# Attention, gated MLP and top-2 experts on one core: TensorE in a fixed order, attention and gate work placed by product count, and a written order for the first four attention tiles

## The chip, the cores and the metric

The kernel runs on one core of a Trainium2 chip. The metric is the device time of one execution in microseconds, as the median of several runs. Five engines work side by side, each through its own list of instructions in order: TensorE (PE; its weight loads are shown apart as PEld), VectorE (DVE), ScalarE (ACT), GpSimd (POOL) and SyncE (SP), whose queue issues nearly all transfers. Engines wait for each other only where data or a buffer demands it.

## The reference, cut to what matters

```python
# attention in chunks of 64: q, k, v are (4, 8, 576, 64)
scores = scale * q_c @ k_c.T;  scores -= scores.max(-1);  attn = exp(scores)
out = (attn / (attn.sum(-1) + 1e-9)) @ v_c          # -> x: 2304 x 512
h = x @ w_in                                        # 512 -> 2048
x = (h * clip(h + 3, 0, 6) / 6) @ w_out             # 2048 -> 512
noisy = x @ w_gate + log1p(exp(x @ w_noise)) * noise
top2, weights = two largest of 8 experts, softmax over the two
out[rows of e] += weight * (relu(x[rows] @ w1[e]) @ w2[e])   # 512 -> 1024 -> 512, e = 0..7
```

## The kernel before, in words

The 2304 tokens are 18 tiles of 128 rows, in five blocks of 4, 4, 4, 3 and 3 tiles (BT). For each block the MLP runs over 16 units of 128 hidden columns. One unit is 12 matmuls into `h` (`s1`, line 230, 512 or 384 columns wide) and 3 matmuls per tile into that tile's accumulator `acc` (`s2`, line 239). Every number is kept as a high and a low part, which is why each product takes three matmuls (PASSES). The `acc` products of unit u are written behind the `h` products of unit u + 1; between them ACT and DVE turn `h` into `r` (L264, L265) and into `g`, high on ACT (L266) and low on DVE (L271).

The MLP weights come as 32 half units of 512 KB in a 64-bit format. During block 0 each half is turned into two float parts: three integer operations on DVE (L141 to L143, into `u`), a copy on ACT (the high part, L145) and a subtraction on DVE (the low part, L154). The even half of a unit is needed by its `h` products, the odd half by its `acc` products.

The attention of a tile is a chain over three engines: scores on PE (`sc`, L166), row maximum on DVE (L168), either eight exponentials with sums on ACT (L174, the form called `acts`) or a subtraction on DVE, one exponential on ACT and a sum on DVE (L176 to L178), the norm on DVE (L183 to L185), four transposes on PE (`pt`, L192) and a copy on ACT (L194), the product with v on PE (`xo`, L209), and the high and low part of the MLP's input on ACT and DVE (L212, L213). Tiles 0 to 3 come ahead of block 0 (the lead phase); the tiles of block b + 1 are worked off during block b. The gate of a tile of the block before is a second chain: transposes (L300), four small products (L309), a transpose (L318), a sum on DVE (L319), and per block a top-2 choice on DVE (`gate_top`) and positions by two small matmuls on PE (`gate_pos`, L369 and L370). The `x2` and `x2e` tiles are what a block hands to its gate. PSUM banks p6 and p7 form the tile `pair`, in which these chains work.

What sets the order: the program is built by a scheduler, which places each engine's instructions by its own estimate of when they can run. Only from block 4 on, up to the second group of expert rows, is TensorE held to the written order (`manual_schedule`). Work beside the MLP is hung in two ways: by unit (`side`), and, in `route`, by `ticks`, a counter that goes up with every 4 `h` matmuls and with every 3 `acc` matmuls. After block 4 come the experts, whose rows are gathered by POOL.

Of the kernel before, what the change touches and what calls it, by code (L numbers as in the profile page):

```python
# [42 lines left out]
def tile_kernel(ctx, tc, qkv, w1u, w2u, wg, noise, out):  # L43
# [115 lines left out]
    def att_a(t, tag, acts=False):  # L159
        qt, kt, vt = st["qkv", t]  # L160
        sc = bank(tag, [P, 8, 64], "sc")
        for c in range(2):
            for hp in range(KD):
                for r in range(2):
                    s = slice(r * 64, r * 64 + 64)
                    nc.tensor.matmul(sc[s, c * KD + hp, :], qt[s, hp, c, :], kt[s, c, hp, :], start=True, stop=True)  # L166
# [4 lines left out]
        if acts:  # L171
            nc.vector.tensor_scalar(mx, mx, -0.125, None, op0=ALU.mult)
            for h in range(8):
                nc.scalar.activation(sm[:, h], sc[:, h], AF.Exp, scale=0.125, bias=mx[:, h], accum_out=su[:, h])  # L174
        else:
            nc.vector.tensor_tensor(sm, sc, mx.to_broadcast([P, 8, 64]), op=ALU.subtract)  # L176
# [20 lines left out]
    def att_c(t):
        b = max(i for i in range(NB) if B0[i] <= t)
        i = t - B0[b]
# [12 lines left out]
        nc.scalar.activation(hi, xo, AF.Copy)  # L212
        nc.vector.tensor_tensor(lo, xo, hi.bitcast(F32), op=ALU.subtract)  # L213
# [289 lines left out]
    warm = bank("p3", [P, 4, P], "warm")  # L503
    for i in range(10):
        nc.tensor.matmul(warm, ones, ones[:, None, :].to_broadcast([P, 4, P]), start=True, stop=True)
# [264 lines left out]
```

## Time and profile before

| | |
|---|---|
| median of 3 runs | 1024.29 us (1023.94 to 1024.99) |
| the profiled execution, own time | 1015.68 us |
| its span, first to last instruction | 1013.9 us |
| its mean granted TensorE clock | 0.966 of full speed |
| DVE, ACT, POOL busy | 434.0, 338.8, 141.9 us |

Times in the rows are microseconds from the start of the span. A timeline row gives start, length, engine, line, operation, the tile written and the tiles read, and a count; equal instructions in a row are merged. In brackets stands how long the engine was idle before, and what released it. The count of small products is doubled or quadrupled there against the program. The length of a group of matmuls overlaps with the next by about 0.1 to 0.4 us, so costs are read from start to start. A row of windows gives, for a stretch, its length, the busy time and number of instructions of each engine, the granted TensorE clock (PEclk) and the use of the DMA engines.

### The profile page before, as it was taken

How to read it: one execution, taken by the hardware profiler on the slowest of the kernel's cores; microseconds unless marked ns; L12 is line 12 of the kernel's file. 1: busy time of each engine (PE TensorE's matmuls, PEld its weight loads, DVE VectorE, ACT ScalarE, POOL GpSimd, SP SyncE). 2: the span in 40 equal slices, each digit the busy share in tenths (PEclk: the TensorE clock that was granted, in tenths of full speed). 3: DMA queues.
4: the chain of work that ended last, by engine and by line, in shares of the span. 5: the costliest groups of instructions: out<-in, count | busy, mean ns of one | idle time of the engine just before them, and what ended most of it. 6: DMA issues, size and time to landing. Idle time of an engine off the chain costs nothing.

```text
span 1013.9 us, 14516 instructions
## 1 busy us (share of the span) xinstructions
PE 958.5 (95%) x5960; PEld 818.6 (81%) x5960; DVE 434.0 (43%) x864; ACT 338.8 (33%) x646; POOL 141.9 (14%) x129
## 2 busy tenths in 40 slices
PE   5699999997999999968999999999999999999995
PEld 3488877775787788857998889898989999999894
DVE  6999542334432343326553343333434343332221
ACT  4355442233222232334552343332333232321110
POOL 0000000000300002004202420221313031130311
PEclk8699999998899999978999999999999999999998
DMA  9555120014910120112531573363736345240412
GB/s 349 197 166 182 64 74 1 32 32 142 275 32 5 48 95 1 32 53 63 155 112 68 101 222 92 110 131 106 131 108 134 105 111 129 74 63 22 52 23 32
DMA packets 37195, 99.46 MB, mean 98 GB/s; under 512 B 9984, under 2 KB 10368, under 8 KB 37120
## 3 DMA queue, kind: packets, MB, share of 16 engines
q1 hardware_dynamic: 27008, 77.43, 24.5%
q0 software_dynamic: 10112, 21.02, 11.6%
q8 instruction: 48, 0.79, 0.3%
q14 instruction: 27, 0.22, 0.1%
HBM read 75.15 MB, written 23.28 MB: 97 GB/s over the span
## 4 chain that ended last, share of the span: by engine, by line
PE 91%; DVE 4%; DMA 1%; ACT 1%; issue 1%; POOL 1%; SPq 0%; POOLq 0%; ACTq 0%
PE h L230 42%; PE acc L239 38%; PE pair L239 3%; PE pair L413 2%; PE pair L166 2%; PE pair L209 1%; PE pair L300 1%; PE pair L309 1%; DMA raw<-in_w1u_dram 1%; PE pair L192 1%; DVE u L142 1%; DVE u L143 0%; POOL table L386 0%; DVE Xa L213 0%; DVE u L141 0%
## 5 line engine op out<-in xcount | busy, mean ns | idle before, releaser
L239 PE MATMUL acc<-w,g 128*128 128x512 f32 x1680 | 430.6, 398 | 0.0
L239 PEld LDWEIGHTS acc<-w,g 128*128 128x128 f32 x1680 | 310.3, 189 | 63.2 <-issue 1.6
L230 PE MATMUL h<-Xa,w 128*128 128x320 f32 (+3 forms) x1344 | 257.6, 341 | 4.5 <-ACT Xa L212 3.8
L230 PEld LDWEIGHTS h<-Xa,w 128*128 128x128 f32 x1344 | 220.2, 192 | 26.3 <-ACT Xa L212 4.3
L118 DVE TENSOR_TENSOR w<-raw,w 128x1024 fp32r<-128x1024 f32 x64 | 78.4, 1226 | 128.7 <-ACT w L117 128.5
L430 DVE SCALAR_TENSOR_TENSOR g<-h,g 128x320 fp32r<-128x320 f32 (+2 forms) x128 | 62.5, 489 | 160.8 <-ACT g L429 160.7
L429 ACT ACTIVATE g<-h 128x320 fp32r<-128x320 f32 (+2 forms) x128 | 56.1, 438 | 201.4 <-PE h L230 201.2
L230 PE MATMUL h<-Xe,w 128*128 128x320 f32 (+1 forms) x672 | 110.3, 316 | 0.0
L265 DVE SCALAR_TENSOR_TENSOR r<-r,h 128x512 f32<-128x512 f32 (+1 forms) x80 | 50.6, 632 | 137.4 <-ACT r L264 137.2
L230 PE MATMUL h<-Xb,w 128*128 128x384 f32 (+1 forms) x480 | 106.8, 366 | 1.4 <-ACT Xb L212 1.4
L230 PEld LDWEIGHTS h<-Xe,w 128*128 128x128 f32 x672 | 103.6, 188 | 2.7
L117 ACT ACTIVATE w<-raw 128x1024 fp32r<-128x1024 f32 x64 | 67.9, 1060 | 100.4 <-PE pair L239 88.1
L264 ACT ACTIVATE r<-h,b 128x512 f32<-128x512 f32 (+1 forms) x80 | 51.6, 645 | 134.2 <-PE h L230 131.2
L230 PEld LDWEIGHTS h<-Xb,w 128*128 128x128 f32 x480 | 85.8, 188 | 13.2 <-ACT Xb L212 1.7
L386 POOL DMA_INDIRECT table<-pay,slot x36 | 36.0, 1000 | 399.8 <-DVE slot L383 390.3
L403 POOL DMA_INDIRECT xr<-x2d,tab x40 | 39.9, 998 | 270.7 <-PE pair L413 252.1
L451 POOL DMA_INDIRECT out_dram<-arena,tab x40 | 63.1, 1576 | 88.0 <-DVE arena L448 68.5
L271 DVE TENSOR_TENSOR g<-r,g 128x512 fp32r<-128x512 f32 (+1 forms) x80 | 50.9, 636 | 38.7 <-ACT g L266 38.0
L266 ACT ACTIVATE g<-r 128x512 fp32r<-128x512 f32 (+1 forms) x80 | 47.2, 590 | 55.7 <-DVE r L265 48.2
L239 PE MATMUL pair<-w,g 128*128 128x512 f32 x144 | 41.7, 395 | 0.0
L239 PEld LDWEIGHTS pair<-w,g 128*128 128x128 f32 x144 | 26.9, 188 | 6.0
L145 ACT ACTIVATE w<-u 128x512 fp32r<-128x512 f32 x32 | 20.1, 632 | 34.0 <-DVE u L143 33.9
(135 smaller groups left out, 527.3 us busy)
## 6 DMA issues: line engine op xcount, KB each, us to landing
raw<-in_w2u_dram SPq DMA_DIRECT2D x64, 512.0 KB, 4.1
raw<-in_w1u_dram SPq DMA_DIRECT2D x24, 512.0 KB, 4.5
arena<-in_qkv_dram SPq DMA_DIRECT2D x14, 768.0 KB, 5.3
out_dram<-zero SPq DMA_DIRECT2D x4, 1536.0 KB, 19.9
rawx<-in_w1u_dram SPq DMA_DIRECT2D x8, 512.0 KB, 8.6
x2d<-x SPq DMA_DIRECT2D x15, 256.0 KB, 2.7
lead<-in_qkv_dram SPq DMA_DIRECT2D x3, 768.0 KB, 9.2
x2d<-zero SPq DMA_DIRECT2D x1, 1536.0 KB, 9.1
```

Source lines behind the costliest of these rows:

```text
L117: nc.scalar.activation(w[:, 0], raw, AF.Copy)
L118: nc.vector.tensor_tensor(w[:, 1], raw, w[:, 0].bitcast(F32), op=ALU.subtract)
L230: nc.tensor.matmul(dst, w[:, a, kd * P:(kd + 1) * P], x[:, b, kd, t0:t0 + n], start=(k == 0), stop=(k == 3 * KD - 1))
L239: nc.tensor.matmul(acc[i], g[:, a, i * P:(i + 1) * P], w[:, b, DM:], start=(first and j == 0), stop=(last and j == 2))
L264: nc.scalar.activation(r, st["h", b], AF.Relu, bias=b3)
L265: nc.vector.scalar_tensor_tensor(r, r, 6.0, st["h", b], op0=ALU.min, op1=ALU.mult)
L266: nc.scalar.activation(st["g", b, u][:, 0], r, AF.Copy)
L271: nc.vector.tensor_tensor(g[:, 1], st["r", b], g[:, 0].bitcast(F32), op=ALU.subtract)
L403: nc.gpsimd.indirect_dma_start(out=xr, out_offset=None, in_=x2d[:rows], in_offset=bass.IndirectOffsetOnAxis(ap=st["tab", key][:, i, 0:1], ...
L429: nc.scalar.activation(g[:, 0, t0:t0 + n], h, AF.Relu)
L430: nc.vector.scalar_tensor_tensor(g[:, 1, t0:t0 + n], h, 0.0, g[:, 0, t0:t0 + n].bitcast(F32), op0=ALU.max, op1=ALU.subtract)
L451: s = nc.gpsimd.indirect_dma_start(out=out, out_offset=bass.IndirectOffsetOnAxis(ap=tab[:, i, 0:1], axis=0), in_=y, in_offset=None, comput ...
```

## The change

The attention and conversion helpers are cut into single steps (`conv_a` into `conv_u` and `conv_hi`, `conv_b` into `conv_lo`, `att_a` into `att_sc`, `att_mx`, `att_e` and `att_n`, `att_b` into `att_pt` and `att_at`, `att_c` into `att_xo`, `att_hi` and `att_lo`). The lead phase is then written out step by step, and PE, DVE and ACT are held to that order among these steps. Between the steps stand 20 more matmuls on constants (`keep_warm`). Only halves 0 and 1 belong to the lead phase now, where there were four; tile 1 takes the exponentials on ACT too; the loads of tiles 1 to 3 go ahead of the first weights. Banks p2 and p5 become a second pair, so that two tiles can have their `xo` at once.

From block 0 on TensorE follows the written order, and the attention and gate steps of blocks 0 to 3 hang on ticks: a tile every 24 ticks (20 where a block has 3 tiles), `pt` 11 ticks behind `sc`, `xo` 4 behind that, the gate of a tile 2, 6 and 9 ticks behind `sc`. DVE, ACT, POOL and SP are still ordered by the scheduler after the lead phase. In the changed file the lines stand further down: L142 to L144 and L159 are the conversion on DVE, L177 to L201 the softmax, L248 the low part of the MLP's input, L305 and L311 `r` and the low part of `g`, L270 and L279 the `h` and `acc` products, L171, L214 and L235 `sc`, `pt` and `xo`, L340, L349 and L358 the gate's steps on PE, L409 and L410 `gate_pos`; `pair_69` and `pair_70` are the two pairs.

```diff
...
-    pair = ps.tile([P, 2, DM], F32, name="pair")
+    pairs = [ps.tile([P, 2, DM], F32, name=f"pair{i}") for i in range(2)]
+    in_pair = {"p6": (0, 0), "p7": (0, 1), "p2": (1, 0), "p5": (1, 1)}
     def bank(tag, shape, name):
-        if tag in ("p6", "p7"):
-            t = pair[:, tag == "p7"]
+        if tag in in_pair:
...
+            t = pairs[in_pair[tag][0]][:, in_pair[tag][1]]
...
-    def conv_a(s):
+    def conv_u(s):
...
-        hi = st["w", "m", j][:, 0, h * DM:(h + 1) * DM]
-        nc.scalar.activation(hi, u.bitcast(F32), AF.Copy)
...
+    def conv_hi(s):
+        if s >= 2 * U1:
+            return
+        j, h = divmod(s, 2)
+        nc.scalar.activation(st["w", "m", j][:, 0, h * DM:(h + 1) * DM], st["u", s].bitcast(F32), AF.Copy)
+    def conv_lo(s):
...
-    def att_a(t, tag, acts=False):
+    def att_sc(t, tag):
...
+    def att_mx(t, acts):
+        sc = st["sc", t]
...
+    def att_e(t):
+        sm, su, mx, acts = st["att", t]
+        sc = st.pop(("sc", t))
+        if acts:
             for h in range(8):
                 nc.scalar.activation(sm[:, h], sc[:, h], AF.Exp, scale=0.125, bias=mx[:, h], accum_out=su[:, h])
         else:
-            nc.vector.tensor_tensor(sm, sc, mx.to_broadcast([P, 8, 64]), op=ALU.subtract)
             nc.scalar.activation(sm, sm, AF.Exp, scale=0.125)
+    def att_n(t):
+        sm, su, mx, acts = st["att", t]
+        if not acts:
...
+    def att_a(t, tag, acts):
+        att_sc(t, tag)
+        att_mx(t, acts)
+        att_e(t)
+        att_n(t)
...
+    def att_pt(t, tag):
...
+    def att_at(t, at):
+        nc.scalar.activation(at, st.pop(("pt", t)), AF.Copy)
         st["attT", t] = at
-    def att_c(t):
-        b = max(i for i in range(NB) if B0[i] <= t)
-        i = t - B0[b]
+    def att_b(t, tag):
+        att_pt(t, tag)
+        att_at(t, at_[0])
+    def att_xo(t, pair=0):
...
+    def att_hi(t):
+        nc.scalar.activation(xpart(t, 0), st["xo", t], AF.Copy)
+    def att_lo(t):
+        nc.vector.tensor_tensor(xpart(t, 1), st.pop(("xo", t)), xpart(t, 0).bitcast(F32), op=ALU.subtract)
+    def att_c(t):
+        att_xo(t)
+        att_hi(t)
+        att_lo(t)
...
-    warm = bank("p3", [P, 4, P], "warm")
-    for i in range(10):
-        nc.tensor.matmul(warm, ones, ones[:, None, :].to_broadcast([P, 4, P]), start=True, stop=True)
+    warm = bank("p4", [P, 4, P], "warm")
+    def keep_warm(n):
+        for i in range(n):
+            nc.tensor.matmul(warm, ones, ones[:, None, :].to_broadcast([P, 4, P]), start=True, stop=True)
+    keep_warm(10)
...
-    for c in [0, 10, 1, 2, 11, 3, 12, 13, 14, 15, 16]:
+    for c in [0, 1, 2, 3, 10, 11, 12, 13, 14, 15, 16]:
...
+    with tc.manual_schedule(engines={nc.tensor.engine, nc.vector.engine, nc.scalar.engine}):
+        att_sc(0, "p0"), att_mx(0, True), att_e(0)
+        att_sc(1, "p1"), att_mx(1, True), att_e(1)
+        keep_warm(3)
+        att_n(0), att_pt(0, "p3"), att_at(0, at_[0])
+        att_sc(2, "p0"), att_mx(2, True)
+        keep_warm(3)
+        att_n(1), att_e(2), att_pt(1, "p3"), att_xo(0, 0), att_at(1, at_[1])
+        att_sc(3, "p1"), att_mx(3, False)
+        att_hi(0), att_e(3), att_xo(1, 1)
+        keep_warm(6)
+        conv_u(0)
+        att_lo(0), att_hi(1), conv_hi(0), att_n(2), att_n(3)
+        att_pt(2, "p3"), att_at(2, at_[0]), att_pt(3, "p3"), att_at(3, at_[1])
+        att_lo(1), att_xo(2, 0), att_xo(3, 1)
+        keep_warm(8)
+        conv_u(1), att_hi(2), conv_hi(1), att_hi(3)
+        conv_lo(0), conv_lo(1)
+        att_lo(2), att_lo(3)
+    constants()
     LT = BT[0]
-    HL = 4
-    step = 0
-    for t in range(LT + 2):
-        if t < LT:
-            att_a(t, ("p0", "p1")[t % 2], t % 2 == 0)
-        if 0 <= t - 2 < LT:
-            att_c(t - 2)
-        if t < LT:
-            att_n(t)
-        if 0 <= t - 1 < LT:
-            att_b(t - 1, ("p2", "p5")[t % 2], at_[t % 2])
-        if step < HL:
-            conv_a(step)
-            if step > 0:
-                conv_b(step - 1)
-            step += 1
-        if t == 1:
-            constants()
-    conv_b(step - 1)
...
-                for s in (2 * u + HL, 2 * u + HL + 1):
-                    conv_a(s)
-                    conv_b(s)
+                for s in (2 * u + 2, 2 * u + 3):
+                    conv_u(s)
+                    conv_hi(s)
+                    conv_lo(s)
...
+    order = tc.manual_schedule(engines={nc.tensor.engine})
+    order.__enter__()
     for b in range(NB):
         side = {}
         if b == 0:
             at(side, 6, table_init)
-        elif b < NB - 1:
+        n0 = st.get("tick", 0)
+        every = 24 if BT[b] == 4 else 20
+        if 0 < b < NB - 1:
             t0, nt = GRP[b - 1]
             for i in range(nt):
-                at(side, 4 * i + 1, gate_t, t0 + i, "p7")
-                at(side, 4 * i + 2, gate_m, t0 + i, "p6")
-                at(side, 4 * i + 2, gate_r, t0 + i, "p6")
-            at(side, 4 * nt - 1, gate_top, b - 1)
-            at(side, 4 * nt - 1, gate_pos, b - 1)
+                n = n0 + 8 + every * i
+                at(ticks, n, gate_t, t0 + i, "p7")
+                at(ticks, n + 4, gate_m, t0 + i, "p7")
+                at(ticks, n + 7, gate_r, t0 + i, "p7")
+            at(ticks, n + 8, gate_top, b - 1)
+            at(ticks, n + 22, gate_pos, b - 1)
...
-                u = 4 * i
-                at(side, u, att_a, t, "p6", b == 0)
-                at(side, u, att_n, t)
-                at(side, u + 2, att_b, t, "p7")
-                at(side, u + 3, att_c, t)
+                n = n0 + 6 + every * i
+                at(ticks, n, att_a, t, "p6", b == 0)
+                at(ticks, n + 11, att_b, t, "p7")
+                at(ticks, n + 15, att_c, t)
                 if t + 2 < NTILE:
-                    at(side, u + 3, load_tile, t + 2, bufs[4 + t % 2])
+                    at(ticks, n + 16, load_tile, t + 2, bufs[4 + t % 2])
         if b == NB - 2:
             for j in range(3):
                 at(side, 12 + j, load_raw, U1 + j)
         if b == NB - 1:
-            order = tc.manual_schedule(engines={nc.tensor.engine})
-            order.__enter__()
...
```

TensorE where block 3 ends and block 4 begins (`Xb` is the input of block 3, `Xa` that of block 4), before:

```order
L239 MATMUL acc<-w,g 128x512 x9
L192 MATMUL pair<-ident,arena 128x128 x4
L209 MATMUL pair<-at_93,arena 64x64 x16
L166 MATMUL pair<-arena 64x64 x16
L300 MATMUL pair<-ident,x_2945 128x128 x4
L309 MATMUL pair<-at_94,wg_sb 32x128 x4
L318 MATMUL pair<-ident,lp 128x128
L192 MATMUL pair<-ident,arena 128x128 x4
L209 MATMUL pair<-at_93,arena 64x64 x16
L230 MATMUL h<-Xa,w 128x384
L300 MATMUL pair<-ident,x2e 128x128 x4
L230 MATMUL h<-Xa,w 128x384 x11
```

and changed:

```order
L270 MATMUL h<-Xb,w 128x384 x12
L279 MATMUL acc<-w,g 128x512 x6
L409 LDWEIGHTS upper
L409 MATMUL pair_69<-m,upper 128x32
L410 LDWEIGHTS ones
L410 MATMUL pair_69<-macc,ones 128x32
L279 MATMUL pair_70<-w,g 128x512 x3
L270 MATMUL h<-Xb,w 128x384 x12
L279 MATMUL acc<-w,g 128x512 x6
L279 MATMUL pair_70<-w,g 128x512 x3
L270 MATMUL h<-Xa,w 128x384 x12
L279 MATMUL acc<-w,g 128x512 x6
```

The last `xo` of one tile and the whole of the next tile's attention, with two gates between, stood in a run without MLP products; now the MLP products of both blocks follow each other, and only `gate_pos` stands among them.

VectorE in the lead phase, before (`u` and `w` are weight conversion, the rest attention):

```order
L141 TENSOR_SCALAR u<-raw 128x512
L142 SCALAR_TENSOR_TENSOR u<-raw,u 128x512
L168 TENSOR_REDUCE mx<-sc 128x8
L143 SCALAR_TENSOR_TENSOR u<-raw,u 128x512
L172 TENSOR_SCALAR mx<-mx 128x8
L154 TENSOR_TENSOR w<-u,w 128x512
L168 TENSOR_REDUCE mx<-sc 128x8
L183 TENSOR_SCALAR su<-su 128x8
L176 TENSOR_TENSOR lead<-sc,mx 128x512
L184 RECIPROCAL su<-su 128x8
L141 TENSOR_SCALAR u<-raw 128x512
L185 TENSOR_TENSOR lead<-lead,su 128x512
```

and changed:

```order
L177 TENSOR_REDUCE mx<-sc 128x8
L181 TENSOR_SCALAR mx<-mx 128x8
L177 TENSOR_REDUCE mx<-sc 128x8
L181 TENSOR_SCALAR mx<-mx 128x8
L199 TENSOR_SCALAR su<-su 128x8
L200 RECIPROCAL su<-su 128x8
L201 TENSOR_TENSOR lead<-lead,su 128x512
L177 TENSOR_REDUCE mx<-sc 128x8
L181 TENSOR_SCALAR mx<-mx 128x8
L199 TENSOR_SCALAR su<-su 128x8
L200 RECIPROCAL su<-su 128x8
L201 TENSOR_TENSOR lead<-lead,su 128x512
```

The conversion steps have left this stretch; they come behind the maximum of tile 3.

VectorE late in block 0, around the `r` of unit 10, before:

```order
L142 SCALAR_TENSOR_TENSOR u<-raw,u 128x512
L271 TENSOR_TENSOR g<-r,g 128x512
L142 SCALAR_TENSOR_TENSOR u<-raw,u 128x512
L143 SCALAR_TENSOR_TENSOR u<-raw,u 128x512 x2
L141 TENSOR_SCALAR u<-raw 128x512
L265 SCALAR_TENSOR_TENSOR r<-r,h 128x512
L142 SCALAR_TENSOR_TENSOR u<-raw,u 128x512
L154 TENSOR_TENSOR w<-u,w 128x512 x2
L168 TENSOR_REDUCE mx<-pair 128x8
L143 SCALAR_TENSOR_TENSOR u<-raw,u 128x512
L271 TENSOR_TENSOR g<-r,g 128x512
```

and changed, around the `r` of the same unit:

```order
L142 TENSOR_SCALAR u<-raw 128x512
L143 SCALAR_TENSOR_TENSOR u<-raw,u 128x512 x2
L159 TENSOR_TENSOR w<-u,w 128x512
L144 SCALAR_TENSOR_TENSOR u<-raw,u 128x512 x2
L142 TENSOR_SCALAR u<-raw 128x512
L159 TENSOR_TENSOR w<-u,w 128x512
L143 SCALAR_TENSOR_TENSOR u<-raw,u 128x512
L159 TENSOR_TENSOR w<-u,w 128x512
L305 SCALAR_TENSOR_TENSOR r<-r,h 128x512
L144 SCALAR_TENSOR_TENSOR u<-raw,u 128x512
L248 TENSOR_TENSOR Xb<-pair_69,Xb 128x2x2x128
L311 TENSOR_TENSOR g<-r,g 128x512
```

Ten of the conversion steps that now stand in a row ahead of this `r` are shown; before, four stood between it and the last `g`.

More of the change, by code (lines that the diff above doesn't have):

```diff
@@ L143, in conv_a @@
         nc.vector.scalar_tensor_tensor(u, lo32, 29, u, op0=ALU.logical_shift_right, op1=ALU.bitwise_or)
-        hi = st["w", "m", j][:, 0, h * DM:(h + 1) * DM]
-        nc.scalar.activation(hi, u.bitcast(F32), AF.Copy)
         st["u", s] = u
         load64(s + 7 if s < 10 else s + 3 if s >= 14 else -1)
-    def conv_b(s):
+    def conv_hi(s):
[4 more added lines that the diff above has]
+    def conv_lo(s):
         if s >= 2 * U1:
@@ L166, in att_a @@
                     nc.tensor.matmul(sc[s, c * KD + hp, :], qt[s, hp, c, :], kt[s, c, hp, :], start=True, stop=True)
+        st["sc", t] = sc
+    def att_mx(t, acts):
+        sc = st["sc", t]
         mx = work.tile([P, 8, 1], F32, tag="mx", bufs=2, name="mx")
@@ L172, in att_a @@
             nc.vector.tensor_scalar(mx, mx, -0.125, None, op0=ALU.mult)
+        else:
+            nc.vector.tensor_tensor(sm, sc, mx.to_broadcast([P, 8, 64]), op=ALU.subtract)
+        st["att", t] = (sm, su, mx, acts)
+    def att_e(t):
+        sm, su, mx, acts = st["att", t]
+        sc = st.pop(("sc", t))
+        if acts:
             for h in range(8):
@@ L175, in att_a @@
         else:
-            nc.vector.tensor_tensor(sm, sc, mx.to_broadcast([P, 8, 64]), op=ALU.subtract)
             nc.scalar.activation(sm, sm, AF.Exp, scale=0.125)
+    def att_n(t):
+        sm, su, mx, acts = st["att", t]
+        if not acts:
             nc.vector.tensor_reduce(su, sm, axis=AX.X, op=ALU.add)
-        st["att", t] = (sm, su)
-    def att_n(t):
-        sm, su = st["att", t]
         nc.vector.tensor_scalar(su, su, 1e-9, None, op0=ALU.add)
@@ L185, in att_n @@
         nc.vector.tensor_tensor(sm, sm, su.to_broadcast([P, 8, 64]), op=ALU.mult)
-    def att_b(t, tag, at=None):
+    def att_a(t, tag, acts):
[4 more added lines that the diff above has]
+    def att_pt(t, tag):
         sm = st.pop(("att", t))[0].rearrange("p h k -> p (h k)")
@@ L192, in att_b @@
             nc.tensor.transpose(pt[:, m, :], sm[:, m * P:(m + 1) * P], ident)
-        at = at_[0] if at is None else at
-        nc.scalar.activation(at, pt, AF.Copy)
+        st["pt", t] = pt
+    def att_at(t, at):
+        nc.scalar.activation(at, st.pop(("pt", t)), AF.Copy)
         st["attT", t] = at
-    def att_c(t):
-        b = max(i for i in range(NB) if B0[i] <= t)
-        i = t - B0[b]
+    def att_b(t, tag):
+        att_pt(t, tag)
+        att_at(t, at_[0])
+    def att_xo(t, pair=0):
         at = st.pop(("attT", t))
         qt, kt, vt = st.pop(("qkv", t))
-        xo = pair[:, :, :2 * P].rearrange("p a (j n) -> p a j n", j=2)
+        xo = pairs[pair][:, :, :2 * P].rearrange("p a (j n) -> p a j n", j=2)
         for c in range(2):
@@ L210, in att_c, with xpart @@
                                          at[s, c * 2 + j, r * 64:r * 64 + 64], start=True, stop=True)
-        hi, lo = (xb[b][:, w, :, i * P:(i + 1) * P].rearrange("p (j a) n -> p a j n", a=2) for w in range(2))
-        nc.scalar.activation(hi, xo, AF.Copy)
-        nc.vector.tensor_tensor(lo, xo, hi.bitcast(F32), op=ALU.subtract)
+        st["xo", t] = xo
+    def xpart(t, w):
+        b = max(i for i in range(NB) if B0[i] <= t)
+        i = t - B0[b]
+        return xb[b][:, w, :, i * P:(i + 1) * P].rearrange("p (j a) n -> p a j n", a=2)
+    def att_hi(t):
[6 more added lines that the diff above has]
+        att_lo(t)
     ticks = {}
```

## Prediction

> **What bounds the kernel now.** I read the head of the page first, then stretches of the span by engine, then TensorE's timeline where it is idle.
>
> ```profile
> span 1013.9 us, 14516 instructions
> ...
> PE 958.5 (95%) x5960; PEld 818.6 (81%) x5960; DVE 434.0 (43%) x864; ACT 338.8 (33%) x646; POOL 141.9 (14%) x129
> ...
> PEclk8699999998899999978999999999999999999998
> ```
>
> TensorE is the bound: 55 of 1014 us are without it, and the clock row drops at the start, in the 10th and 11th slice and in the 18th and 19th (each 25.3 us). What is to be won lies there. Everywhere else TensorE runs at these rates:
>
> ```profile
> 71.41 2.77 PE h L230 x12
> ...
> 117.96 2.78 PE acc L239 x12
> ...
> 359.75 4.06 PE L230 MATMUL h<-Xb,w 128*128 128x384 f32 x22
> 363.74 0.43 PE L309 MATMUL pair<-at,wg_sb 128*32 128x128 f32 x8
> ```
>
> 12 products of 512 columns in 2.77 or 2.78 us are 0.231 each; from 359.75 to 363.74 stand 22 of 384 columns, 0.181 each.
>
> First, the lead phase and block 0. The third column group is TensorE, then weight loads, then DVE:
>
> ```profile
> 8.50:21.50 13.00, 7.32 (x136) 6.30 (x136) 11.34 (x26) 7.21 (x36) 0.00 (x0) 0.74 1.03 414
> 21.50:41.60 20.10, 6.94 (x107) 4.99 (x107) 20.10 (x41) 8.69 (x15) 0.00 (x0) 0.57 0.79 290
> 41.60:110.00 68.40, 68.40 (x431) 55.05 (x432) 66.92 (x127) 34.48 (x84) 1.89 (x4) 0.98 0.48 152
> ...
> 110.00:142.10 32.10, 31.43 (x225) 25.12 (x223) 11.49 (x21) 14.48 (x47) 0.00 (x0) 1.00 0.10 31
> ...
> L154 DVE TENSOR_TENSOR w<-u,w x32: 673/682/693, 11.6 to 109.2; 128x512 fp32r<-128x512 f32 x32
> ```
>
> DVE is busy 98.4 of the 101.5 us up to 110 (11.34 + 20.10 + 66.92), where its last weight conversion ends (the last L154 starts at 109.2), and 11.5 of 32.1 us behind that. So up to 110 two engines are at their limit at once from 41.6 on, and DVE alone before. TensorE enters block 0 late and cold:
>
> ```profile
> 1.07 4.45 PE L505 MATMUL warm<-ones 128*128 128x512 bf16 x10 [1.07 <-DVE early L522]
> ...
> 10.40 1.93 PE L166 MATMUL sc<-lead 64*64 64x64 f32 x32 [3.08 <-DMA lead<-in_qkv_dram]
> ...
> 15.87 1.11 PE L192 MATMUL pt<-ident,lead 128*128 128x128 f32 x4
> ...
> 39.65 1.22 PE L230 MATMUL h<-Xa,w 128*128 128x512 f32 x2 [2.33 <-ACT Xa L212]
> 41.58 4.18 PE L230 MATMUL h<-Xa,w 128*128 128x512 f32 x11 [0.71 <-DVE Xa L213]
> ...
> 142.14 3.56 PE L230 MATMUL h<-Xb,w 128*128 128x512 f32 x13 [0.71 <-ACT Xb L212]
> ```
>
> Second, where block 1 ends. From 242.14 to 256.79 no MLP product runs; the steps of one tile's attention wait for each other, and the clock is halved by the time the products return:
>
> ```profile
> 242.14 0.69 PE L209 MATMUL pair<-at,arena 64*64 64x64 f32 x32
> 244.27 1.15 PE L166 MATMUL pair<-arena 64*64 64x64 f32 x32 [1.44 <-DVE Xa L213]
> 246.94 1.12 PE L300 MATMUL pair<-ident,x2e 128*128 128x128 f32 x4 [1.52 <-DVE arena L176]
> ...
> 256.79 4.58 PE L230 MATMUL h<-Xa,w 128*128 128x512 f32 x13 [0.72 <-ACT Xa L212]
> 261.30 1.15 PE L166 MATMUL pair<-arena 64*64 64x64 f32 x32
> ...
> 256.00:260.00 4.00, 3.28 (x12) 2.55 (x9) 0.69 (x1) 0.60 (x1) 3.08 (x4) 0.54 1.02 416
> 260.00:264.00 4.00, 4.00 (x45) 3.14 (x45) 1.83 (x3) 1.32 (x2) 3.09 (x4) 1.00 1.07 391
> ```
>
> Third, the same where block 3 ends, from 431.46 to 469.93, with a second wait in it, for the top-2 choice:
>
> ```profile
> 431.46 0.60 PE L192 MATMUL pair<-ident,arena 128*128 128x128 f32 x4
> ...
> 458.63 0.18 PE L369 MATMUL pair<-m,upper 128*128 128x32 bf16 x1 [3.45 <-DVE m L349]
> ...
> 468.05 0.42 PE L309 MATMUL pair<-at,wg_sb 128*32 128x128 f32 x8 [0.32 <-DVE lgs L319]
> ...
> 469.93 2.34 PE L239 MATMUL acc<-w,g 128*128 128x512 f32 x9
> ...
> 458.00:462.00 4.00, 2.65 (x10) 2.00 (x9) 2.10 (x16) 0.71 (x2) 1.03 (x2) 0.50 0.02 4
> ```
>
> The 3.45 us without work before 458.63 are followed by a halved clock (0.50). The Trainium skill ("TensorE: Matmul & The Clock Gate", "What's actually happening") has the clock fall to half after an idle window of about 3.4 us and come back after a busy one; these rows agree.
>
> **The boundaries.** What the steps cost among products, at full clock, is read from start to start:
>
> ```profile
> 63.01 0.60 PE L192 MATMUL pair<-ident,arena 128*128 128x128 f32 x4
> 63.37 2.57 PE L239 MATMUL acc<-w,g 128*128 128x512 f32 x10
> ...
> 68.66 0.69 PE L209 MATMUL pair<-at,arena 64*64 64x64 f32 x32
> 69.28 2.13 PE L239 MATMUL acc<-w,g 128*128 128x512 f32 x8
> ...
> 76.45 1.15 PE L166 MATMUL pair<-arena 64*64 64x64 f32 x32
> 77.53 0.73 PE L239 MATMUL acc<-w,g 128*128 128x512 f32 x2
> ```
>
> `pt` costs 0.36, `xo` 0.62, `sc` 1.08. A `gate_t` is the same four transposes, 0.36; `gate_m` I put at 0.36 too; the transpose of `gate_r` and `gate_pos` at under 0.1 each.
>
> End of block 1: 242.14 to 261.30 are 19.2 us. In them lie two `xo`, one each of `sc`, `pt`, `gate_t`, `gate_m`, `gate_r` and `gate_pos` (3.5) and 13 products of 0.231 (3.0). In the new order these steps stand among products some ticks earlier, and the products of block 2 follow those of block 1. 19.2 − 6.5: **−12.7 us**. The cover is the product work between the ticks: 11 ticks from `sc` to `pt` are some 9 us (11/7 of a unit of 5.55), and the chain that ran bare took 2.7 from `sc` through the subtraction (244.27 to 246.94) and needs one exponential and two full-width DVE steps more, some 5 us in all.
>
> End of block 3: 431.46 to 469.93 are 38.5 us. The rows of the stretch add up to two `pt`, two `xo`, one `sc`, five each of `gate_t`, `gate_m` and `gate_r` and one `gate_pos` (6.9), 36 `h` products of 384 columns (6.5) and 18 `acc` products (4.2): 17.6. That leaves 20.9. The three gates that `route` hangs at the head of block 4 stay as dense as they are; one such wait is 0.32 (the row at 468.05), and I leave 0.9 for them: **−20.0 us**.
>
> End of block 2: there is one gap like the 0.71 at 142.14: **−0.7 us**.
>
> **The lead phase.** The new order of DVE holds no conversion until the maximum of tile 3. I follow its chain: tile 1's scores waited for its load until 10.40, with a 0.5 MB weight load ahead in the queue that now comes later; at the 414 GB/s or so that the DMA moved this is 1.3 us, so 9.1. Then at half clock, as the PE rows of this phase have it (granted were 0.74 and 0.57 in the first two windows): `sc` 1.9, maximum with its scaling 0.8, norm of tile 0 0.9, `pt` 1.1, `sc` 1.9, maximum 0.8, norm 0.9, `pt` 1.1, `xo` the same, `sc` 1.9. A full-width step of DVE has these rows, 0.67 long and 0.60 from start to start (the shift 0.41 and 0.34):
>
> ```profile
> 61.12 0.67 DVE L265 SCALAR_TENSOR_TENSOR r<-r,h 128x512 f32<-128x512 f32 x1
> 61.72 0.67 DVE L154 TENSOR_TENSOR w<-u,w 128x512 fp32r<-128x512 f32 x1
> 62.32 0.41 DVE L141 TENSOR_SCALAR u<-raw 128x512 int32<-128x512 int32 x1
> 62.66 0.67 DVE L154 TENSOR_TENSOR w<-u,w 128x512 fp32r<-128x512 f32 x1
> ```
>
> So the maximum of tile 3 starts at 21.5; at full clock the six PE steps take half, 17.2. Behind it DVE is never out of work: to the end of tile 3's low part (`att_lo`), which block 0 waits for, stand 19 full-width steps, 5 shifts and 4 small ones, 19 × 0.60 + 5 × 0.34 + 0.4 = 13.5. TensorE enters block 0 at 35, or 31 at full clock, against 41.6: taken alone, 7 to 11 us gained, with 1.6 of cold products at 41.58 (11 in 4.18 instead of 2.54). The 20 added warm-up products are paid for by waits that are there anyway, the longest run, the last eight, by the wait for that low part; bare it would cost 3.6 (ten took 4.45 at 1.07).
>
> **Why I do not count that gain.** DVE does the same work as before but idles longer at the start: up to 21.5 it has 4.4 us of work (three maxima and two norms of 0.68, six small steps of under 0.2) where it did 11.3. All of the work up to the last conversion, 98.4 us, remains (tile 1 loses two steps of 0.68, tile 6's norm and low part are drawn in instead). 21.5 + 98.4 − 4.4 is 115.5; with a third of the 1.5 us of gaps of the third window row, 116. The changed order puts the low part of unit 10's `g` 0.6 us ahead of the last conversion, and TensorE cannot go on with the `acc` products of unit 10 without it. What TensorE then has to do is 10 + 4 × 12 + 12 `acc` products, four runs of 12 `h`, one `sc`, `pt` and `xo`: 2.3 + 11.1 + 2.8 + 11.1 + 2.1 = 29.4. So block 0 is done at 115.4 + 29.4 = 144.8, against 142.1: **+2.7 us**, from −1.6 (full clock in the lead phase) to +6 (weight loads late by 3 us; three buffers of one kind serve the later halves). TensorE, earlier by 7 us, waits about 11 us within block 0 instead, at `acc` (for `g`) and at `pt` (for the norm).
>
> **The hung steps.** 10 tiles and 12 gates in blocks 1 to 3 bring 66 places at which PE now stops if a chain is late. Where the distance is 4 ticks or more nothing waits (3 us for a 0.6 us copy). At 2 or 3 ticks (`gate_m` to `gate_r` to `pt`) the nearest row is the 0.32 at 468.05, in an order already fixed, against 0.00 elsewhere: 0 to 0.32 on 22 places, 0 to 7 us; I take **+2.0**, nearer to nothing since DVE and ACT are idle for more than half of these blocks.
>
> **The sum.** −12.7 − 20.0 − 0.7 + 2.7 + 2.0 = −28.7. The profiled execution took 1015.7, 1.8 more than its span, and would take 987. The median of the runs shown is 8.6 above it; I carry that over: 1024.3 − 28.7, **996 us**. Behind block 4 nothing of weight changes: TensorE's order was fixed there already or stays the scheduler's.
>
> **The rivals.**
>
> The lead gain survives: DVE's list is read too strictly, and block 0 ends 8 us or more earlier than I say, at 134 to 137. For it speaks that TensorE alone needs only 16 × 5.55 + 8.2 from 35. Against it, DVE's 98.4 us. It gives 996 − 9, 987.
>
> Block 0 becomes worse: DVE's order runs ten or more conversions ahead of a waiting `r`, so single waits reach 3.5 to 4 us (a `pt` behind a norm that stands behind two units' conversions). A wait of 3.45 halved the clock above; a halved clock cost 1.5 at 256.79 (13 products in 4.51 instead of 3.00) and half of the 4 us of the row of 458 is 2 and more. Three of these at 2.3 and late loads of 3: +10, 1006. By the Trainium skill's rule of the idle window (above) it needs waits of over 3.4 us, and I have two near that.
>
> The other side: the fixed order makes TensorE stand at every hung step. At 66 places the sum of −28.7 is used up at 0.43 us each beyond the 2.0 that I count; `route`'s 0.32 on all of them (21, for my 2) would leave −10, and 0.6 (40) gives +9, 1033. Against it: chains of 5 us have 9 us of cover. The Trainium skill ("TensorE: Matmul & The Clock Gate", "Architectural detail: the array is 16× 32×32, not 1× 128×128") lets PE pull only weight loads ahead of products, so it could not step around such a wait.
>
> That the change does not do what it says: `pair_70` now carries two accumulators, and if its halves wait for each other, `acc` evictions delay every block. The order shows `acc` products unbroken, so I give it little; the time would be near 1024.
>
> **How the numbers follow.** My case 0.62; the lead gain survives 0.14; block 0 worse 0.16; standing at each step 0.05; nothing 0.03. The likeliest alone has 988 to 1003. The range takes in the second and third case: 982 to 1009. A change under 0.2% (2 us) is about what a measurement of this kernel cannot tell from none. Faster 0.92, same 0.03, slower 0.05.
>
> **What would show it.** Right: no stretch of 10 us without MLP products where blocks 1 and 3 end, no clock of 0.50 between 60 and the end; first `h` products at 31 to 36; DVE busy without gap from about 21 to 115; PE waiting some 11 us in block 0 for L311 and L201. Wrong: block 0 over by 136, or PE waits of 0.3 us and more at most gate steps.

## The result, and the profile after

The changed kernel takes 997.16 us (median of 4, 996.79 to 997.49) beside 1024.61 for the kernel before (median of 4, 1023.94 to 1024.99): a ratio of 0.9733, interval 0.9716 to 0.975. The profiled execution took 996.98, with a span of 995.2.

The kernel before has two levels: about 1025 us in two sets of runs and about 1016 in two others (the runs of one set share a chip). The profile that the prediction reads, 1015.7, is of the lower level, its timed runs are of the upper one.

The head of the page after the change: span, busy time of each engine, and granted clock in 40 slices.

```profile
span 995.2 us, 14562 instructions
...
PE 955.8 (96%) x5980; PEld 811.2 (82%) x5980; DVE 433.6 (44%) x863; ACT 338.9 (34%) x661; POOL 141.7 (14%) x129
...
PEclk8899899999999999999999999999999999999998
```

The drops in the 10th, 11th, 18th and 19th slice are gone. Where blocks 1 and 3 end, the windows (TensorE's busy time first, the clock behind the engines) are full, but for the gates at the head of block 4:

```profile
225.00:250.00 25.00, 25.00 (x147) 19.54 (x146) 11.11 (x47) 7.84 (x16) 3.33 (x3) 1.00 0.11 32
250.00:275.00 25.00, 25.00 (x176) 19.64 (x175) 10.79 (x18) 8.31 (x15) 6.32 (x7) 1.00 0.66 253
425.00:450.00 25.00, 22.67 (x136) 18.80 (x135) 7.85 (x19) 9.37 (x18) 8.10 (x8) 1.00 0.10 33
450.00:475.00 25.00, 25.00 (x128) 22.41 (x127) 16.49 (x48) 12.80 (x22) 5.85 (x6) 1.00 0.40 109
```

Block 0 is the other way round. Before, TensorE was busy for 68.40 of the 68.40 us from 41.6 to 110. Now it is busy for 56.63, and the clock drops in the middle of a block that had none of that:

```profile
41.60:110.00 68.40, 56.63 (x345) 44.01 (x345) 65.34 (x128) 33.63 (x92) 0.76 (x3) 0.94 0.50 166
110.00:142.10 32.10, 32.10 (x221) 25.60 (x220) 16.76 (x30) 13.10 (x33) 0.00 (x0) 0.96 0.22 67
```

TensorE's waits from 41.6 to 160, and one of them followed through TensorE and DVE (scores, maximum, the norm's three steps, transposes):

```profile
PE pair L214 <- DVE arena L201: 9.3, 3, 4.8
PE acc L279 <- DVE g L311: 2.3, 2, 1.7
```

```profile
63.02 1.15 PE L171 MATMUL pair<-arena 64*64 64x64 f32 x32
66.26 0.68 DVE L177 TENSOR_REDUCE mx<-pair 128x8 f32<-128x512 f32 x1
72.92 0.16 DVE L199 TENSOR_SCALAR su<-su 128x8 f32<-128x8 f32 x1
74.80 0.19 DVE L200 RECIPROCAL su<-su 128x8 f32<-128x8 f32 x1
76.20 0.68 DVE L201 TENSOR_TENSOR arena<-arena,su 128x512 f32<-128x512 f32 x1
77.03 0.63 PE L214 MATMUL pair<-ident,arena 128*128 128x128 f32 x4 [3.68 <-DVE arena L201]
```

From the scores to the end of the norm 13.9 us pass (63.02 to 76.88), because conversions, `r` and `g` stand between the steps on DVE; TensorE comes to `pt` 10.3 us behind the scores (77.03 − 3.68 − 63.02). Two waits are long enough to be followed by half the clock:

```profile
78.30:81.70 3.40, 3.40 (x10) 2.37 (x8) 3.40 (x9) 0.53 (x1) 0.00 (x0) 0.52 0.15 57
105.60:112.40 6.80, 5.16 (x15) 4.23 (x16) 6.80 (x14) 2.18 (x4) 0.00 (x0) 0.51 0.55 189
```

### The profile page after: what moved, and what is told of

Its sections match the earlier page's. It is cut to its first block, busy times and chain, and to the rows that moved or that the text cites. A ratio compares the mean times of both kernels' runs of the same rounds, so it can differ in the third digit from the quotient of the medians.

```text
span 995.2 us, 14562 instructions
## 1 busy us (share of the span) xinstructions
PE 955.8 (96%) x5980; PEld 811.2 (82%) x5980; DVE 433.6 (44%) x863; ACT 338.9 (34%) x661; POOL 141.7 (14%) x129
## 4 chain that ended last, share of the span: by engine, by line
PE 87%; DVE 8%; DMA 2%; issue 1%; ACT 1%; POOL 0%; SPq 0%; DVEq 0%; ACTq 0%; POOLq 0%
PE h L270 41%; PE acc L279 21%; PE pair L279 19%; PE pair L453 2%; DMA raw<-in_w1u_dram 2%; DVE u L144 1%; DVE u L143 1%; PE pair L340 1%; PE pair L171 1%; DVE u L142 1%; PE pair L235 1%; DMA lead<-in_qkv_dram 1%; DVE g L311 1%; DVE r L305 1%; PE pair L349 1%
## 5 line engine op out<-in xcount | busy, mean ns | idle before, releaser
L279 PE MATMUL acc<-w,g 128*128 128x512 f32 x960 | 262.4, 398 | 2.5 <-DVE g L311 2.3
L270 PE MATMUL h<-Xa,w 128*128 128x320 f32 (+3 forms) x1344 | 251.7, 337 | 1.8 <-DVE Xa L248 1.7
L279 PE MATMUL pair<-w,g 128*128 128x512 f32 x864 | 235.3, 400 | 0.8 <-ACT at L341 0.8
L270 PEld LDWEIGHTS h<-Xa,w 128*128 128x128 f32 x1344 | 217.0, 189 | 22.7 <-DVE Xa L248 2.0
L279 PEld LDWEIGHTS acc<-w,g 128*128 128x128 f32 x960 | 174.3, 188 | 35.2 <-DVE g L311 3.2
L279 PEld LDWEIGHTS pair<-w,g 128*128 128x128 f32 x864 | 161.5, 190 | 38.3 <-ACT at L341 1.3
L270 PE MATMUL h<-Xe,w 128*128 128x320 f32 (+1 forms) x672 | 110.2, 315 | 0.0
L270 PE MATMUL h<-Xb,w 128*128 128x384 f32 (+1 forms) x480 | 106.6, 366 | 0.0
L305 DVE SCALAR_TENSOR_TENSOR r<-r,h 128x512 f32<-128x512 f32 (+1 forms) x80 | 50.6, 632 | 126.4 <-ACT r L304 117.5
L270 PEld LDWEIGHTS h<-Xe,w 128*128 128x128 f32 x672 | 103.5, 188 | 2.5
L270 PEld LDWEIGHTS h<-Xb,w 128*128 128x128 f32 x480 | 85.6, 188 | 11.1 <-issue 0.8
L311 DVE TENSOR_TENSOR g<-r,g 128x512 fp32r<-128x512 f32 (+1 forms) x80 | 50.9, 636 | 32.9 <-ACT g L306 31.6
```

What stands on the lines that cost most here:

```text
L270: nc.tensor.matmul(dst, w[:, a, kd * P:(kd + 1) * P], x[:, b, kd, t0:t0 + n], start=(k == 0), stop=(k == 3 * KD - 1))
L279: nc.tensor.matmul(acc[i], g[:, a, i * P:(i + 1) * P], w[:, b, DM:], start=(first and j == 0), stop=(last and j == 2))
L305: nc.vector.scalar_tensor_tensor(r, r, 6.0, st["h", b], op0=ALU.min, op1=ALU.mult)
L311: nc.vector.tensor_tensor(g[:, 1], st["r", b], g[:, 0].bitcast(F32), op=ALU.subtract)
```

## The experiments

Twelve runs in three sets. Times of different sets are compared by their ratio to the kernel before of the same set: 1025.68 in the first (e1 to e4), 1017.14 in the second (e5 to e8), 1016.24 in the third (e9 to e12).

### Why the profile of before lies below its times

Two profiles of the kernel before, unchanged (e1 and e10), and one of the changed kernel beside the second (e9).

> The kernel before, unchanged, profiled and timed once more. Theory: the time of an execution hangs on where the granted clock goes to half, and the profiled execution that the prediction used was a lucky one: the new profile takes about 1024 us, with some 9 us more between the same products, in stretches where the granted clock is 0.5, and a mean clock of 0.955 or less. Rival: every profiled execution of it takes about 1016 us and every other one about 1024.6 us; then the 9 us belong to the profiling and the two profiles are not to be subtracted.

> The kernel before, one more profile. Theory: where it takes 1015 to 1019 us, VectorE and ScalarE work on during the GpSimd bursts near 380 and 470 us, and TensorE does not wait at the first gate transposes of block 3; where it takes 1023 to 1027 us, both stand until the burst's last instruction ends. Rival: the two times differ by the granted clock alone, with the same waits.

> The changed kernel, unchanged, beside the next three on their chip. The kernel before took 1025 us in one set of runs and 1017 in the other. Theory: the waits that differ between the two sets are waits of the kernel before (VectorE idle to the end of a GpSimd burst, and half clock behind it) that the fixed order does not meet; the changed kernel takes 995 to 999 us beside either. Rival: it moves with the kernel before: 988 to 991 us beside 1017, a constant ratio of 0.973.

Measured: e1 1025.30 us (1024.09 to 1027.14), its profile 1026.45; e10 1016.69, one execution; e9 995.66 (993.69 to 996.09), ratio 0.9791, interval 0.9778 to 0.9805. Block 3 in e1, timeline of GpSimd, VectorE, ScalarE and TensorE: the product that VectorE's and ScalarE's next steps need, the last of eight indirect writes of `gate_pos`, and then these steps.

```profile
384.06 0.44 PE L230 MATMUL h<-Xb,w 128*128 128x384 f32 x1
...
388.88 0.97 POOL L386 DMA_INDIRECT table<-pay,slot  x1 [0.30 <-issue]
390.00 0.69 DVE L168 TENSOR_REDUCE mx<-pair 128x8 f32<-128x512 f32 x1 [8.62 <-PE h L230]
390.10 0.58 ACT L264 ACTIVATE r<-h,b 128x384 f32<-128x384 f32 x1 [9.31 <-PE h L230]
...
391.47 0.66 PE L300 MATMUL pair<-ident,x 128*128 128x128 f32 x4 [2.79 <-DVE arena L176]
391.94 2.10 PE L230 MATMUL h<-Xb,w 128*128 128x384 f32 x6
```

The same steps in e10, where both engines work on during the burst:

```profile
383.73 0.69 DVE L168 TENSOR_REDUCE mx<-pair 128x8 f32<-128x512 f32 x1 [2.79 <-PE pair L166]
384.15 0.58 ACT L264 ACTIVATE r<-h,b 128x384 f32<-128x384 f32 x1 [3.81 <-PE h L230]
...
388.07 0.60 PE L300 MATMUL pair<-ident,x 128*128 128x128 f32 x4
388.42 1.30 PE L230 MATMUL h<-Xb,w 128*128 128x384 f32 x6
388.43 0.97 POOL L386 DMA_INDIRECT table<-pay,slot  x1 [0.30 <-issue]
```

In e1 the two engines stand, from 381 on and for 5.5 us after that product is through, until the burst is over; TensorE waits 2.79 us for them, and its next six products take 2.10 instead of 1.30. The same instructions of the same program ran during the burst in e10, so no data and no buffer of the program holds them in e1: here engines wait for something else besides. At the next burst VectorE stands 5.17 us and TensorE 3.21:

```profile
475.81 0.97 POOL L386 DMA_INDIRECT table<-pay,slot  x1 [0.30 <-issue]
476.90 0.23 DVE L319 TENSOR_REDUCE lgs<-pair 128x16 f32<-128x64 f32 x1 [5.17 <-remote]
477.18 0.42 PE L309 MATMUL pair<-at,wg_sb 128*32 128x128 f32 x8 [3.21 <-DVE lgs L319]
```

So the theory of e10 holds, and that of e1 in its time. Its clock of 0.955 or less did not come: 0.961, against 0.963 in e10, so most of the difference is waiting and not clock. The two stretches in which these bursts lie (between the MLP products number 864, 1344 and 1632, counted as in the table below) are 4.6 and 4.1 us longer in e1 than in e10. The theory of e9 holds too: the changed kernel moves from 997.2 to 995.7 while the kernel before moves by 9. It is not quite free of the stand: TensorE waits 1.6 us at one gate in the set at 1025 and not in the one at 1016. The change is worth 27.4 us at one level and 20.6 at the other. What makes the engines stand in one set and not in the other is not shown; the sets ran on different chips, and nothing here separates the chip from other causes.

### What each part of the change is worth

e2 takes the changed kernel with the lead phase of before, e3 its lead phase with the order and the hanging of before.

```diff
 e2
-for c in [0, 1, 2, 3, 10, 11, ...          written lead phase, conv_u(0), conv_u(1)
+for c in [0, 10, 1, 2, 11, 3, ...          old loop, halves 0 to 3 converted
 e3
-order.__enter__()                          ahead of block 0
+order.__enter__()                          at block 4; side work hung by unit
```

> The changed kernel with the old lead phase (the loop of before, four halves converted ahead of block 0, the old order of loads); the fixed order and the hung steps stay. Theory (VectorE's order in block 0 sets when block 0 ends, so the 7 us of the new lead are lost there): block 0 ends within 3 us of where it ends now, and the time is 994 to 1000 us. Rival 1 (the lead's gain reaches the end): 1004 us, 7 us slower than the changed kernel. Rival 2 (the new lead itself harms block 0, because only two halves are converted when it starts): 987 to 992 us.

> The changed kernel's lead phase, with the scheduler's order and the side work hung by unit in blocks 0 to 3, as before. Theory (what the lead gains is lost in block 0; the gains are the ends of blocks 1 and 3): 1021 to 1028 us, the waits at the ends of blocks 1 and 3 as before, about 12 and 20 us. Rival (the lead's 7 us reach the end): 1016 to 1018 us.

Measured: e2 999.31 us (997.85 to 999.67), ratio 0.9739 (0.9726 to 0.9752); e3 1018.08 (1017.69 to 1019.35), ratio 0.9931 (0.9919 to 0.9944). e2 is as the theory has it: 384 MLP products, as many as block 0 has, are issued by 151.7 with the old lead and by 150.3 with the new one. e3 is a miss. The lead's 7 us reach the end where the scheduler orders block 0, and TensorE has next to no wait there although VectorE is as full as I thought it could be:

```profile
41.60:110.00 68.40, 66.79 (x404) 53.93 (x404) 67.40 (x132) 36.71 (x98) 0.98 (x3) 1.00 0.51 172
```

So a full VectorE alone does not explain block 0. e4 tests its order: VectorE too follows the written order in block 0, with the same work.

```diff
+conv_u(2), conv_hi(2), conv_u(3), conv_hi(3), conv_lo(2)                    (end of the lead phase)
-order = tc.manual_schedule(engines={nc.tensor.engine})                      (block 0)
+order = tc.manual_schedule(engines={nc.tensor.engine, nc.vector.engine})
-for s in (2u + 2, 2u + 3): conv_u(s), conv_hi(s), conv_lo(s)
+conv_u(2u + 4), conv_hi(2u + 4), conv_lo(2u + 3), mlp_lo(u), conv_u(2u + 5), conv_hi(2u + 5), conv_lo(2u + 4)
+at(ticks, n + 6, att_n, t)                                                  (was at n)
```

> The changed kernel with VectorE too held to a written order in block 0: r, a conversion and its low half, g, the next conversion; the softmax's norm written six ticks behind its scores. The work is the same. Theory (it is VectorE's scheduled order, conversions ahead of r, g and the norm, that makes TensorE wait in block 0): the waits at pt and at acc (11.5 us together) go, and with them the two stretches of half clock (10 us at 0.5, 5 us lost); block 0 ends 8 to 15 us earlier, and the time is 982 to 989 us. Rival (VectorE's amount of work binds block 0: 82 us of it in the 100 us from 41.6 to 142): 994 to 1000 us, with the waits moved to h or to w. Second rival: a strict order stalls VectorE behind ScalarE, over 1000 us.

Measured: 997.29 us (996.27 to 997.93), ratio 0.9727 (0.9714 to 0.9739). The theory is refuted: the time is that of the changed kernel. The waits for the low part of `g` are gone, but the waits at `pt` are still there, though VectorE's last conversion now starts 19 us later (138.5 against 119.6):

```profile
PE pair L214 <- DVE arena L201: 9.8, 4, 4.8
```

The time lies in the range of the first rival, but the waits did not move to `h` or `w` as it has it, so this run does not show that VectorE's amount of work binds. e5 leaves VectorE to the scheduler and moves `pt` by five ticks (called counts from here on):

```diff
+d = 5 if b == 0 else 0
-at(ticks, n + 11, att_b, t, "p7"); at(ticks, n + 15, att_c, t)
+at(ticks, n + 11 + d, att_b, t, "p7"); at(ticks, n + 15 + d, att_c, t)     (and the load behind it)
```

> The changed kernel with pt, xo and the load behind them hung five counts later in block 0 alone (16 and 20 counts behind the scores instead of 11 and 15). Theory (TensorE reaches pt too early for a VectorE that is full; the place of pt is what costs): the three waits at pt (9.3 us) and the half clock behind them (5 us) go: 984 to 990 us. Rival (a fixed TensorE order runs into the full VectorE wherever pt stands: the waits move to acc and h): 994 to 999 us.

Measured: 982.77 us (981.89 to 984.35), ratio 0.9669 (0.9651 to 0.9687). Scores and transposes of the tile that waited, and the window:

```profile
61.21 1.15 PE L171 MATMUL pair<-arena 64*64 64x64 f32 x32
...
75.56 0.60 PE L214 MATMUL pair<-ident,arena 128*128 128x128 f32 x4
...
41.60:110.00 68.40, 65.05 (x448) 50.69 (x447) 65.77 (x128) 35.21 (x96) 1.15 (x3) 1.00 0.52 170
```

14.35 us between them, and no wait at `pt`. From 41.6 on there remain 2.7 us of waits for `g` (1.5 and 1.2) and 0.6 us at one `sc` in block 0. The theory holds, and the rival does not, since the waits did not move: the place of `pt` costs, five counts of it some 12 us by the ratios (0.9669 against e9's 0.9791).

e6 goes back to the scheduler's order and to units in block 0 alone; e7 takes the old lead phase besides.

```diff
-order.__enter__()                                   ahead of block 0
+if b == 1: order.__enter__()
+if b == 0: at(side, 4 * i, att_a, ...), at(side, 4 * i + 2, att_b, ...), at(side, 4 * i + 3, att_c, t)
```

> The changed kernel, but block 0 is hung by unit and its order left to the scheduler, as before; blocks 1 to 3 keep the fixed order and the counts. Theory (the fixed order costs in block 0, because there VectorE has 97% of its time filled; lead and block ends are additive gains): block 0's 384 products end at 133 us as in the run with the new lead alone, instead of 148, and this stays to the end: 980 to 985 us. Rival 1 (VectorE's work left over from block 0 is met again by the hung steps of block 1): 988 to 995 us. Rival 2 (the waits in block 0 were of no account at the end of block 1): 996 to 998 us.

> The same with the old lead phase too: what is left of the change is the fixed order and the counts in blocks 1 to 3. Theory (where TensorE keeps no fixed order in block 0, the lead's 6 to 7 us reach the end): 986 to 991 us. Rival (the lead's gain shows only together with the scheduler's order in all blocks): within 2 us of the run before it.

Measured: e6 980.89 us (980.18 to 982.21), ratio 0.9651 (0.9633 to 0.9668); e7 988.72 (987.66 to 989.97), ratio 0.9724 (0.9706 to 0.9742). Both theories hold. e6 has the lowest time of all, 1.4% under the changed kernel by the ratios of the two sets at 1016 (0.9651 against 0.9791); its interval overlaps that of e5. Its TensorE comes to `pt` 14.3 us behind the scores, as in e5, and has 1.5 us of waits from 140 to 470:

```profile
68.81 1.15 PE L171 MATMUL pair<-arena 64*64 64x64 f32 x32
...
83.11 0.60 PE L214 MATMUL pair<-ident,arena 128*128 128x128 f32 x4
...
41.60:110.00 68.40, 68.28 (x410) 55.14 (x411) 67.14 (x131) 36.82 (x98) 0.98 (x3) 1.00 0.50 165
```

```profile
PE pair L340 <- DVE arena L183: 0.9, 3, 0.4
PE pair L349 <- DVE lgs L359: 0.3, 1, 0.3
PE pair L279 <- ACT at L341: 0.3, 1, 0.3
```

At the lower level the parts are then: fixed order and counts in blocks 1 to 3 −28.4 (1017.1 to e7), the lead phase −7.8 (e7 to e6), fixed order and counts in block 0 +14.8 (e6 to e9, which is of another set; 14.2 by the ratios). The last part hangs on the place of `pt`: with five counts more (e5) it is 1.9.

### The fixed order or the counts

In blocks 1 to 3, with block 0 left free: e8 keeps the fixed order and hangs by unit, e11 keeps the counts and lets the scheduler order.

```diff
 e8
-at(ticks, n + 8 ..., gate_t), at(ticks, n + 12 ..., gate_m), ...
+at(side, 4 * i + 1, gate_t), at(side, 4 * i + 2, gate_m), at(side, 4 * i + 2, gate_r), ...
 e11
-if b == 1: order.__enter__()
+if b == NB - 1: order.__enter__()
```

> As the run with block 0 free, but in blocks 1 to 3 the side work is hung by unit, as before, under the fixed TensorE order. Theory (the fixed order pays only with the steps spread by count: in one unit gate_m and gate_r stand right behind gate_t and pos right behind the gate's chain on VectorE): some 0.7 us for each of 8 gated tiles and 4 to 6 us for each pos, 18 to 28 us over the run with block 0 free: 1000 to 1010 us. Rival (the fixed order alone makes the gain): 980 to 987 us.

> As the run with block 0 free, but with the scheduler's order in blocks 1 to 3 as well; the side work stays hung by count there. With it the four cells are complete: order (scheduler, fixed) by hanging (unit, count) in blocks 1 to 3. Theory (both are needed: the count spreads the steps, and the fixed order keeps the scheduler from gathering them again at the block's end): 6 to 20 us over the run with block 0 free, 987 to 1001 us. Rival (the counts alone make the gain): 980 to 984 us.

Measured, with e3 as the fourth cell, as ratios to the kernel before (intervals of ±0.0013 to ±0.0022):

| blocks 1 to 3 | hung by unit | by count |
|---|---|---|
| scheduler's order | 0.9931 (e3) | 0.9925 (e11, 1008.83 us) |
| fixed order | 0.9767 (e8, 992.62 us) | 0.9651 (e6, 980.89 us) |

Both expectations miss. Without the fixed order the counts are worth nothing: e11 is 28 us over e6, not 6 to 20. The scheduler has put its steps at the end of block 1 back into one heap:

```profile
237.34 0.69 PE L235 MATMUL pair<-at,arena 64*64 64x64 f32 x32
239.47 1.15 PE L171 MATMUL pair<-arena 64*64 64x64 f32 x32 [1.44 <-DVE Xa L248]
242.14 0.66 PE L340 MATMUL pair<-ident,x2e 128*128 128x128 f32 x4 [1.52 <-DVE arena L183]
...
248.87 1.22 PE L270 MATMUL h<-Xa,w 128*128 128x512 f32 x2 [0.72 <-ACT Xa L245]
...
250.01 6.70 PE L270 MATMUL h<-Xa,w 128*128 128x512 f32 x19
```

From 237.34 to 248.87 there is no MLP product, and then 19 products take 6.70 (4.4 at 0.231 each). The fixed order is worth 17 us by unit (0.9931 to 0.9767) and 28 with the counts. (e3 ran at the upper level and meets the same stand there as the kernel before, VectorE idle for 8.71 us to the end of a burst, so its ratio is taken between two kernels that are held up alike.) The steps spread by count are worth 12 us on top of the fixed order; e8's loss is less than I said, since a step that waits for the one before it costs 0.3 to 0.4 us:

```profile
PE pair L358 <- ACT lp L351: 4.8, 12, 0.4
PE pair L214 <- DVE lgs L359: 3.2, 10, 0.3
```

### The products on ones

e12 is e6 without the 20 products that keep TensorE busy in the lead phase.

```diff
-keep_warm(3)   -keep_warm(3)   -keep_warm(6)   -keep_warm(8)
```

> As the run with block 0 free, without the 20 products on ones that keep TensorE busy in the lead. Theory (VectorE and the transfers set when block 0 starts; the products fill gaps): within 1 us of the run with block 0 free, 980 to 982 us. Rival (without them the transposes of the lead and the first products run at half clock): 2 to 4 us more.

Measured: 985.14 us (984.7 to 987.06), ratio 0.9701 (0.9688 to 0.9715). The rival was right, a little over its range: 4.2 us by the medians, 5.1 by the ratios, which compare across sets. First e12, then e6, by windows:

```profile
18.00:23.00 5.00, 4.62 (x100) 4.09 (x100) 1.17 (x2) 2.40 (x12) 0.00 (x0) 0.50 1.04 407
...
33.00:38.00 5.00, 3.00 (x33) 2.35 (x33) 4.97 (x11) 1.46 (x3) 0.00 (x0) 0.50 0.65 221
```

```profile
18.00:23.00 5.00, 3.32 (x102) 2.29 (x98) 3.41 (x6) 3.05 (x11) 0.00 (x0) 1.00 1.03 404
...
33.00:38.00 5.00, 5.00 (x48) 3.98 (x48) 5.00 (x11) 1.20 (x2) 0.00 (x0) 1.00 0.46 156
```

Without them the clock is 0.50 from 13 to 38; the last scores come 2.3 us later, VectorE's chain with them, and block 0 starts at 36.7 instead of 32.5. The products do not fill gaps only: they shorten the small steps on which VectorE waits. The scores account for 2.3 of the 4.2 us; the rest comes behind them and was not followed step by step.

## Why the prediction was right or wrong

The table has the times at which TensorE goes on to its next MLP product after so many (each instruction of the trace counted once), for e10 and e9, which share a set. Block 0 has 384 of them; 864 lies behind the end of block 1, 1632 behind the head of block 4.

| MLP products | before (e10) | changed (e9) | change in the stretch | forecast |
|---|---|---|---|---|
| 0 (lead phase) | 39.8 | 32.8 | −7.0 | |
| 384 (block 0) | 143.0 | 151.3 | +15.3 | with the lead +2.7 |
| 864 (end of block 1) | 284.0 | 282.8 | −9.5 | −12.7 |
| 1632 (ends of blocks 2 and 3) | 491.6 | 470.2 | −20.2 | −20.7 |
| end of the span | 1014.9 | 994.1 | +0.6 | 0 |

The forecast has 2.0 for the hung steps besides, spread over the rows 864 and 1632.

- **The block ends were right** in place and size: −12.7 and −20.7 with +2.0 make a forecast of −31.4, measured −29.7. e11 shows that it is the fixed order that takes them away.
- **The hung steps** cost 1.5 us (e6, 140 to 470), forecast 2.0. The rival of a stop at each of them did not come; hung by unit, the fixed order costs 12 more (e8).
- **The lead phase** was right: 35 forecast, 34.43 for the first run of `h` products, 31 to 36 for the first of them and 32.3 measured.
- **Block 0 was wrong**: with the lead +8.3 (e9 against e10; +8.1 between the two profiles shown), forecast +2.7 in a range to +6. The step that failed is "DVE does the same work as before but idles longer at the start", from which I concluded that block 0 ends 29.4 us behind the last conversion. The amount is real: the last conversion starts at 119.6 now (109.2 before, forecast end 115.5), later than forecast because VectorE also waits 4.5 us for weight loads where I put 0.5 for gaps. TensorE has issued 384 products 30.7 us behind it, close to the 29.4, but that agreement is no cause: in e5 the last conversion starts at 120.4 and the 384 products are through 17 us later, at 137.4; in e6 it starts at 120.3 and they are through 16 us later. The last conversion in the changed kernel, its waits for loads, and the last conversion in e5:

```profile
119.61 0.68 DVE L159 TENSOR_TENSOR w<-u,w 128x512 fp32r<-128x512 f32 x1
```

```profile
DVE u L142 <- DMA raw<-in_w1u_dram: 4.5, 5, 1.5
```

```profile
120.38 0.69 DVE L159 TENSOR_TENSOR w<-u,w 128x512 fp32r<-128x512 f32 x1
```

What costs is the place of `pt`. I gave it 11 counts, "some 9 us", against a chain of "some 5 us in all", which is the chain on an idle VectorE; I used that cover for block 1 and did not work it out for block 0, where the chain takes 13.9. That TensorE would wait for L201 and L311, 11 us in all, was right (11.6); that these waits only took the place of others was not, and my sign of no clock of 0.50 behind 60 failed with them (0.52 and 0.51). The rival "block 0 worse" had this mechanism, a `pt` behind a norm behind conversions with half clock behind it. It gave it 10 us on top of my +2.7; 5.6 came, so the right mechanism stood among the rivals, and its size lay between that rival's and mine.
- **The offset** was wrong: "I carry that over" took the 8.6 us between profile and median as constant. It is a set of waits of the kernel before, and the changed kernel loses most of them: −20.6 at the lower level, −27.4 at the upper. Against the spans of e10 and e9 my −28.7 is 8 too much (5.6 in block 0, the rest at the block ends and behind them); against the medians it is right within 1.3 us, because this excess and the 6.8 us of additional gain at the upper level nearly cancel. 996 is right by luck: a sum with two wrong terms.
- **The lead gain survives** was put at 987 and set aside on VectorE's 98.4 us. e3, e6 and e7 show that it does survive where block 0 is left to the scheduler: 7.6 to 7.8 us. With `pt` held at 11 counts it is lost (e2), as I forecast, but not for the reason that I gave.
- **The two accumulators in one tile** cost next to nothing, but their halves do wait for each other: twice, in block 4 (447.21) and behind it, an `acc` in `pair_70` waits up to 0.4 us for ScalarE (L341) to read a gate's transposes out of the other half, 0.8 us in all; the kernel before has no such wait.

## What to carry to other kernels

Before an engine is held to a written order, take for each hung step the length of its chain on the engines as they are filled at that place, not on idle ones: 5 us became 14 on a VectorE that is 96% busy, and five counts more were worth 1.2% of the kernel. Where a second engine is full, a fixed order costs if a hung step comes too early; here the scheduler's order and a later place did about equally well (e6 and e5). A fixed order pays where stretches of dependent steps heap up, and it may be chosen block by block. Take the kernel before from more than one set of runs before a difference between its profile and its median is carried into a sum.
